# Gradients of four interleaved layers on one core: sums behind a block, loads in another order, three banks for small transposes

## The chip, the cores and the metric

The kernel runs on one core of a Trainium2 chip. The metric is device time in microseconds (us) of one execution; before the change the median of three runs is 1201.8 us (1201.69 to 1202.94). Its engines are named as in the profile: PE (TensorE, matmuls and transposes), DVE (VectorE), ACT (ScalarE), POOL (GpSimd) and SP (SyncE, which here issues DMA transfers). Accumulators of PE lie in PSUM banks, all other tiles on the chip in SBUF; DRAM holds inputs, outputs and what is saved for the gradients.

## The reference: what is computed

Input x has 2048 rows of 512, in bfloat16. Four layers follow one another, each adding to x, and the kernel returns the output and the gradients of all inputs for a given grad_out:

```python
x = x + A(layernorm(x))      # layer 0
x = x + B(layernorm(x))      # layer 1
x = x + A(layernorm(x))      # layer 2, same weights
x = x + B(layernorm(x))      # layer 3, same weights
# A: qkv = h @ wqkv; 32 heads of 16; phi(t) = where(t > 0, t + 1, exp(t)) + 1e-6
#    kv = phi(k)^T v; z = sum phi(k); o = phi(q) kv / (phi(q) z + 1e-6); o @ wo
# B: h = sigmoid(h @ w_gate) * (h @ w_up); h @ w_down       (inner width 1376)
out, vjp = jax.vjp(f, x, wqkv, wo, w_gate, w_up, w_down)
return out, *vjp(grad_out)
```

## The kernel before, in words

**Stages.** The forward layers take the first 430 us or so; they save to DRAM what the gradients need (tensors named sv_...). The gradient stages come in this order, with their approximate times in the profiled execution: `BBwd` of layer 3 (433 to 556 us), `ABwd.first` of layer 2, called A2.first (556 to 638), `ABwd.second` of layer 2 (638 to 716), the rest of layer 3's weight-gradient units and the start of layer 1 (to 780), `BBwd` of layer 1 (780 to 899), A0.first (899 to 980), A0.second (980 to 1060), then small transposes and weight-gradient units that are left (to the end, 1198).

**BBwd** (from L1166; `run` from L1287 on). The 2048 rows are four blocks of 512 (`NBLK`), the inner width of 1376 is eleven units of 128 (`NFC`; the last is 96). For unit n = 11 B + u:

- `D(n)`: four matmuls make the gradient of the inner product, dhh_ps (L1241), in one of two PSUM banks; ACT casts it to the tile dhb (L1247), DVE multiplies the PSUM with one saved factor (L1248) and POOL dhb with the other (L1249), which gives dd. The saved factors ssd are loaded per group of two or three units.
- `R(n)`: once a group is complete, DVE transposes dd in blocks (L924, 1.5 us each) and SP stores it as sv_hdd or sv_hdl, for the weight gradients later.
- `H(B, u)`: eight matmuls (L1273) add the unit's share to the four accumulators dh_ps of the block.
- `ln_begin(B)` follows the last unit of a block. For each accumulator ACT writes t_sb (L1101), DVE makes a sum (tile junk, L1120) and POOL a small factor ab; only then are the four accumulators free. Later steps of the LayerNorm gradient (add_t, add_r) are spread over the next block's units.

`D` runs two units ahead of `H` (`LOOK`). At the beginning of layer 3 the first units' tiles come from an earlier pool (names pre_...), because they are made before `run` opens its pools; dhb of the units in `run` comes from pool bb_work, whose memory the last forward stores (out_t) used. At the end of `run`, `nxt.gT_make`, `nxt.dp_make` and `nxt.start` do the first steps of the ABwd stage that follows, and `next(fill)` issues a fill unit.

**Fill units.** `p_set` holds a set of operands of weight gradients (rows of sv_hdd, sv_hdl or sv_dqk, 1 to 1.5 MB, two buffers), `p_a` the other operand of the whole length. A unit is 16 matmuls (p_ps, L1511). Its result goes through dw_stg (DVE L1526 or ACT L1528) to a partial sum in DRAM (dwp_...) or to the output, in the last case through transposes wd_tp (L1486). Fill units stand between the steps of ABwd so that PE has work while other engines work.

**ABwd.first** (L1597). For each of 16 tiles of 128 rows: `dp_make` (L1582, four matmuls), `gT_make` (L1574), `cneg_make`, `dq_ops` on DVE (L1637 to L1643), `accum_dz`, and a fill unit (every fourth tile two for layer 0). `dq_ops` multiplies with the saved query factors, tile phq_ld (256 KB for two tiles, three buffers, loaded through `BatchLoader`, L1153), and overwrites them; after each pair `dqk_store` stores them as sv_dqk in two DMAs (L1543). At its start `load_a_weights` (L243) issues loads of X_Nv (0.5 MB), wqkvT (1.5 MB) and woT (0.5 MB); they are used in `second`, and their tiles share memory with layer B's weights. GT (L1679 ff.) is written into half of the last one. pqn loads follow (three of 0.5 MB), then phq_ld. For layer 2, `b_load_all` loads a2 (p_a, 2 MB in four DMAs) when `open_a2` is called, ahead of `first`; for layer 0 the call stands ahead of A0.first likewise.

**Small transposes** (`a_small_transposes`, L1822): ten groups of four transposes (four of G, four of X, two of kvbd and dkvbd), each group through a tile fin_ps in the single bank "ln", copied out by ACT and DVE in turn (L362, L364), then four stores.

**What orders the work.** In the gradient stages `tc.manual_schedule(engines=EM)` keeps PE, ACT, DVE and POOL in the order in which the Python code issues instructions; SP is not in it, and its DMAs are put in order by the scheduler, with `tc.issue_after(ins)` as a bound. SP has one queue in order: a store that waits for its data holds all loads behind it. At most eight DMAs are outstanding (each issue waits for the landing of the eighth before).

## Time and profile before

| | |
|---|---|
| Median of the runs | 1201.8 us (1201.69 to 1202.94, 3 runs) |
| Profiled execution, its own time | 1199.77 us |
| Span of that execution | 1198.1 us |
| Mean granted clock of PE | 0.994 |
| DMA traffic | 258.18 MB, mean 216 GB/s |

By stretch, us of busy time in the profiled execution:

| Stretch, us | PE | DVE | ACT | POOL | clock | DMA share |
|---|---|---|---|---|---|---|
| 425 to 570, block stage of layer 3 | 137.95 of 145 | 97.54 | 58.80 | 85.81 | 0.99 | 0.80 |
| 570 to 640, A2.first | 68.67 of 70 | 47.96 | 29.98 | 8.74 | 1.00 | 0.73 |
| 640 to 780, A2.second and rest | 138.41 of 140 | 52.92 | 65.75 | 3.07 | 1.00 | 0.67 |
| 780 to 912, block stage of layer 1 | 128.53 of 132 | 92.60 | 64.09 | 83.87 | 1.00 | 0.77 |
| 912 to 985, A0.first | 67.66 of 73 | 52.72 | 28.77 | 8.45 | 1.00 | 0.81 |
| 985 to 1060, A0.second | 74.32 of 75 | 50.37 | 45.39 | 13.37 | 1.00 | 0.48 |
| 1060 to 1076, small transposes | 13.70 of 16 | 3.70 | 4.08 | 0.00 | 0.89 | 0.79 |
| 1076 to 1198, units left | 116.58 of 122 | 26.21 | 7.79 | 0.00 | 0.99 | 0.77 |

A row says how long an engine had instructions running in that stretch. "Clock" is the share of full speed that PE was granted. In lines of the timeline, the bracket at the end tells how long the engine was idle ahead of the instruction and what ended that time; in lines of waits the numbers are total us, times, and the longest.

### The profile page before, as it was taken

The numbers are of one execution on the slowest core, as the hardware profiler recorded it, in microseconds if no ns is written. First come the engines' busy times: TensorE is split into PE (matmuls) and PEld (weight loads), VectorE is DVE, ScalarE is ACT, GpSimd is POOL, SyncE is SP. The second block draws the span as 40 slices with busy tenths as digits, with TensorE's granted clock in tenths as the row PEclk, the third lists the DMA queues.
The fourth block names the chain that finished last, engine by engine and source line by source line (L and its number), as shares of the span: only waits on it lengthen the run. The fifth ranks groups of instructions, "written<-read, shape, count | busy, mean of one in ns | idle before, by whom it ended". The sixth has DMA issues, their size and how long they took to land. (4 is left out here: it accounts for less than half of the span.)

```text
span 1198.1 us, 21274 instructions
## 1 busy us (share of the span) xinstructions
PE 1139.9 (95%) x7958; PEld 699.2 (58%) x8066; DVE 739.8 (62%) x1275; ACT 569.0 (47%) x1039; POOL 412.8 (34%) x578
## 2 busy tenths in 40 slices
PE   7989999997999989999999999999999989999998
PEld 4467776446777644445555556744447645556577
DVE  6688887877767557767684760066777946732221
ACT  5666666546676623444545652245545427620001
POOL 4237775204766435774110000047771101100000
PEclk9999999999999999999999999999999999999999
DMA  7934566534556666879865439987769874459875
GB/s 241 311 121 147 174 192 190 172 131 141 174 168 215 203 224 216 299 225 332 286 219 155 141 107 311 304 305 224 232 203 334 269 229 145 150 175 312 271 209 165
DMA packets 282184, 258.18 MB, mean 216 GB/s; under 512 B 29216, under 2 KB 261600, under 8 KB 280928
## 3 DMA queue, kind: packets, MB, share of 16 engines
q1 hardware_dynamic: 282080, 256.82, 67.0%
q8 instruction: 63, 1.03, 0.3%
q14 instruction: 41, 0.34, 0.1%
HBM read 137.30 MB, written 119.47 MB: 214 GB/s over the span
## 5 line engine op out<-in xcount | busy, mean ns | idle before, releaser
L1511 PE MATMUL p_ps<-p_set,p_a 128*128 128x384 bf16 (+2 forms) x1792 | 268.9, 305 | 7.7 <-DMA p_set<-sv_hdd 3.3
L1511 PEld LDWEIGHTS <-p_a 128*128 128x128 bf16 x1792 | 168.8, 96 | 89.7 <-issue 5.4
L1249 POOL TENSOR_TENSOR dd<-dhb,ssd 128x512 bf16<-128x512 bf16 x85 | 98.2, 1156 | 122.4 <-ACT dhb L1247 120.1
L1248 DVE TENSOR_TENSOR dd<-dhh_ps,ssd 128x512 bf16<-128x512 f32 x85 | 57.6, 678 | 121.0 <-ACT dhb L1247 119.7
L1273 PE MATMUL dh_ps<-wuT,dd 128*128 128x512 bf16 (+1 forms) x340 | 129.0, 379 | 2.9 <-DVE junk L1120 2.0
L972 POOL TENSOR_TENSOR ssd_t<-hhT,oms 128x512 bf16<-128x512 bf16 (+1 forms) x92 | 97.9, 1070 | 75.0 <-DVE hhT L971 30.8
L1273 PE MATMUL dh_ps<-wgT,dd 128*128 128x512 bf16 (+1 forms) x324 | 122.9, 379 | 0.0
L1273 PEld LDWEIGHTS <-dd 128*128 128x128 bf16 x680 | 66.3, 98 | 83.7 <-issue 5.2
L1247 ACT CAST dhb<-dhh_ps 128x512 bf16<-128x512 f32 x86 | 50.3, 587 | 122.2 <-PE dhh_ps L1241 105.2
L955 PE MATMUL g_ps<-hT,wg 128*128 128x256 bf16 (+1 forms) x792 | 93.5, 262 | 1.2 <-DVE hT L362 1.2
L955 PE MATMUL u_ps<-hT,wu 128*128 128x256 bf16 (+1 forms) x792 | 93.3, 262 | 0.5 <-DVE hhT L971 0.5
L1526 DVE TENSOR_TENSOR dw_stg<-p_ps,dw_stg 128x384 bf16<-128x384 f32 (+2 forms) x76 | 32.1, 438 | 99.8 <-PE p_ps L1511 99.4
L924 DVE STREAM_TRANSPOSE tr_stg<-dd 128x768 f32<-128x768 f32 (+1 forms) x62 | 86.8, 1436 | 3.6 <-DMA sv_hdd<-tr_stg 1.7
L971 DVE TENSOR_TENSOR hhT<-u_ps,ssd_t 128x512 bf16<-128x512 f32 (+1 forms) x92 | 57.7, 631 | 49.7 <-ACT ssd_t L969 37.5
L969 ACT ACTIVATE ssd_t<-g_ps 128x512 bf16<-128x512 f32 (+1 forms) x92 | 51.9, 564 | 66.3 <-PE g_ps L955 51.9
L1241 PE MATMUL dhh_ps<-gT,wdT 128*128 128x512 bf16 x302 | 78.3, 379 | 2.0 <-ACT gT L1213 1.1
L987 PE MATMUL y_ps<-wd,hhT 128*128 128x512 bf16 (+1 forms) x337 | 78.7, 380 | 0.8
L955 PEld LDWEIGHTS <-wg 128*128 128x128 bf16 x792 | 69.6, 99 | 16.6 <-issue 0.8
L955 PEld LDWEIGHTS <-wu 128*128 128x128 bf16 x792 | 71.2, 99 | 7.6 <-issue 0.7
L1528 ACT CAST dw_stg<-p_ps 128x384 bf16<-128x384 f32 (+2 forms) x76 | 28.1, 386 | 80.7 <-PE p_ps L1511 76.7
L1241 PEld LDWEIGHTS <-wdT 128*128 128x128 bf16 x352 | 34.0, 98 | 44.9 <-issue 6.9
L987 PEld LDWEIGHTS <-hhT 128*128 128x128 bf16 (+1 forms) x352 | 34.3, 98 | 35.3
(263 smaller groups left out, 2067.4 us busy)
## 6 DMA issues: line engine op xcount, KB each, us to landing
sv_hdd<-tr_stg SPq DMA_DIRECT2D x72, 384.0 KB, 3.8
p_set<-sv_hdd SPq DMA_DIRECT2D x18, 1536.0 KB, 7.2
sv_ssd<-ssd_t SPq DMA_DIRECT2D x74, 256.0 KB, 2.4
ssd<-sv_ssd SPq DMA_DIRECT2D x23, 768.0 KB, 4.8
p_set<-sv_dqk SPq DMA_DIRECT2D x8, 1024.0 KB, 6.9
h_ld<-sv_h SPq DMA_DIRECT2D x30, 256.0 KB, 4.0
sv_hdl<-tr_stg SPq DMA_DIRECT2D x24, 256.0 KB, 4.5
p_a<-sv_h SPq DMA_DIRECT2D x12, 512.0 KB, 6.8
```

What stands on the lines that cost most here:

```text
L924: nc.vector.transpose(t[:, :, 0:n * P].bitcast(F32).rearrange("p q (a j) -> p q a j", a=2 * n), src.rearrange("p c x -> p (c x)").bitcast( ...
L955: nc.tensor.matmul(ps[:, ci * n:(ci + 1) * n], lhsT=w_sb[:, kc, (c0 + ci) * P:(c0 + ci + 1) * P], rhs=hT[:, kc, (st % 2) * P:(st % 2) * P ...
L969: nc.scalar.activation(ssd[:, :, 0, :], gv, ACT.Sigmoid)
L971: nc.vector.tensor_tensor(hh, uv, ssd[:, :, 0, :], ALU.mult)
L972: nc.gpsimd.tensor_tensor(ssd[:, :, 1, :], hh, oms, ALU.mult)
L987: nc.tensor.matmul(y_ps[:], lhsT=h[0:r, fc, off:off + P], rhs=k.wd[0:r, fc, :], start=(fc == 0), stop=(fc == NFC - 1))
L1241: nc.tensor.matmul(ps[:], lhsT=k.wdT[:, jc, u * P:(u + 1) * P], rhs=self.gT[B][:, jc, :], start=(jc == 0), stop=(jc == NDC - 1))
L1247: nc.scalar.copy(dhb[:], ps[:])
L1248: nc.vector.tensor_tensor(self.dd[ng][:, 0, c, :], ps[:], self.ssd[ng][:, c, 0, :], ALU.mult)
L1249: nc.gpsimd.tensor_tensor(self.dd[ng][:, 1, c, :], dhb[:], self.ssd[ng][:, c, 1, :], ALU.mult)
L1273: nc.tensor.matmul(self.acc[j][:], lhsT=dd[0:r, a, c, j * P:(j + 1) * P], rhs=w[0:r, u, :], start=(u == 0 and a == 0), stop=(u == NFC - 1 ...
L1511: nc.tensor.matmul(ps[:, 0:w], lhsT=lhs[:, s, ic * P:(ic + 1) * P], rhs=rhs, start=(s == 0), stop=(s == NST - 1))
```

## The change

Nothing that is computed changes, and no matmul is added or removed; instructions stand in another order, and some tiles in other memory.

- In `D`, units n below 4 of the layer-3 stage put dhb into the earlier pool (pre_dhb).
- `run` makes `D` and `R` of one more unit ahead of the loop. At a block's end the sums (`ln_begin`) follow `H` directly, then two units of `D`; `R` comes behind. In layer 3, block 2, unit 9, `D` follows `H`.
- At the end of `run`: sums of tiles 0 and 1, a fill unit, sums of tiles 2 and 3, then `gT_make(1)`.
- In `first`, phq_ld tiles are loaded by `load_ph` (two pairs ahead of the loop, then two pairs early), pqn behind them, a2 behind the first pqn, and `load_a_weights` at tile 4, behind the factors issued last.
- `a_small_transposes` takes the banks "t", "ln", "t" in turn ("t" has two).

```diff
         def open_a2(l):
             k.a2ctx = ExitStack()
-            ectx = k.a2ctx if l == 3 else bctx
-            k.a2 = b_load_all(k, R, k.sv[l]["gbf"], "p2_a2", ectx.enter_context(
-                tc.tile_pool(name=f"a2_{l}", bufs=1, reuse_waits="tile")))
+            pool = (k.a2ctx if l == 3 else bctx).enter_context(
+                tc.tile_pool(name=f"a2_{l}", bufs=1, reuse_waits="tile"))
+
+            def load():
+                k.a2 = b_load_all(k, R, k.sv[l]["gbf"], "p2_a2", pool)
+            k.load_a2 = load
...
-        if self.p["work"] is None:
+        if self.first and n < 4:
             dhb = k.pre["pool"].tile([P, BT], BF16, name="pre_dhb")
...
-    def ln_begin(self, B):
+    def ln_begin(self, B, js=range(NB)):
...
             for n in range(self.LOOK):
                 self.D(n)
                 self.R(n)
+            self.D(self.LOOK)
+            self.R(self.LOOK)
...
-                    self.D(n + self.LOOK)
-                    if end and u == NFC - 1:
+                    close = u == NFC - 1
+                    behind = self.first and B == 2 and u == 9
+                    if close and end:
                         nxt.gT_make(0, "ln")
+                    if not close and not behind:
+                        self.D(n + self.LOOK)
                     self.H(B, u)
-                    self.R(n + self.LOOK)
+                    if behind:
+                        self.D(n + self.LOOK)
+                    if close and not end:
+                        done = self.ln_begin(B)
+                        for i in range(2):
+                            self.D(n + self.LOOK + i)
+                    if u:
+                        self.R(n + self.LOOK)
+                    if close and not end:
+                        self.R(n + self.LOOK + 1)
...
-                if end:
-                    nxt.gT_make(1, "ln")
-                lns = self.ln_begin(B)
+                if not end:
+                    lns = done
+            lns = self.ln_begin(B, (0, 1))
             next(fill)
+            lns += self.ln_begin(B, (2, 3))
+            nxt.gT_make(1, "ln")
...
-        k.load_a_weights(l)
...
-            phld = BatchLoader(k, stg, sv["phq"], "phq_ld", nb=NB2)
+            phs = {}
+
+            def load_ph(i):
+                if i < NST // NB2:
+                    phs[i] = stg.tile([P, NB2, D], BF16, name="phq_ld")
+                    phs["ins"] = nc.sync.dma_start(out=phs[i][:], in_=dram_batch(sv["phq"], i, NB2)).ins
...
-            for b in range(1, NST // NB):
-                nc.sync.dma_start(out=self.pqn[b][:], in_=dram_batch(sv["pqn"], b))
+            load_ph(0)
+            load_ph(1)
+            with tc.issue_after(phs["ins"]):
+                for b in range(1, NST // NB):
+                    ins = nc.sync.dma_start(out=self.pqn[b][:], in_=dram_batch(sv["pqn"], b)).ins
+                    if b == 1:
+                        with tc.issue_after(ins):
+                            k.load_a2()
             for st in range(NST):
-                ph_st = phld.get(st)
-                T = dict(st=st, ph=ph_st, ph_pair=phld.cur)
+                if st % NB2 == 1:
+                    load_ph(st // NB2 + 2)
+                if st == 4:
+                    with tc.issue_after(phs["ins"]):
+                        k.load_a_weights(l)
+                    GT = k.GT
+                T = dict(st=st, ph=phs[st // NB2][:, st % NB2, :], ph_pair=phs[st // NB2])
...
-        ps = ps_tile(k, "ln", [P, NDC, P], BF16, "fin_ps")
+        ps = ps_tile(k, ("t", "ln", "t")[n % 3], [P, NDC, P], BF16, "fin_ps")
```

In the built order of the changed program, SP's queue in both first stages reads: query factors, pqn, a2 (p_a), the other pqn, p_set, stores of dqk, factors, X_Nv, wqkvT, woT, p_set. At the end of layer 0 nine groups of small transposes stand with two fill matmuls among them.

More of the change, by code (lines that the diff above doesn't have):

```diff
@@ L1274, in H @@
                                  start=(u == 0 and a == 0), stop=(u == NFC - 1 and a == 1))
-    def ln_begin(self, B):
+    def ln_begin(self, B, js=range(NB)):
         k, l = self.k, self.l
         out = []
-        for j in range(NB):
+        for j in js:
             st = B * NB + j
@@ L1283, in ln_begin @@
                              rs, k.xs[st], self.G[B][:, j, :] if self.first else None, bufs=4))
-            out[j].sums_ps(self.acc[j][:], rs)
+            out[-1].sums_ps(self.acc[j][:], rs)
         return out
@@ L1606, in first @@
         small = self.small = ctx.enter_context(tc.tile_pool(name=f"ab_small{l}", bufs=6, reuse_waits="tile"))
-        GT = k.GT
         self.dkvbdT = big.tile([P, NDC, P], BF16, name="dkvbdT")
```

## The prediction, on record

> **What bounds the kernel now.** I began with the page: busy times, then the span in slices.

> ```profile
> PE 1139.9 (95%) x7958; PEld 699.2 (58%) x8066; DVE 739.8 (62%) x1275; ACT 569.0 (47%) x1039; POOL 412.8 (34%) x578
> ...
> PEclk9999999999999999999999999999999999999999
> ```

> PE is busy 95% of 1198.1 us. The change adds and removes no matmul, so only PE's idle time (58 us) and what it runs slowly can change; no other engine is near its limit. Second view, PE's waits (line of the waiting matmul, releaser, total us, times, longest):

> ```profile
> PE dhh_ps L1241 <- DVE pre_dd L1248: 3.6, 1, 3.6
> PE p_ps L1511 <- DMA p_set<-sv_hdd: 3.3, 2, 2.6
> ...
> PE dh_ps L1273 <- DVE junk L1120: 2.0, 7, 0.5
> ...
> PE p_ps L1511 <- ACT dw_stg L1528: 1.2, 2, 1.0
> PE dhh_ps L1241 <- ACT gT L1213: 1.1, 1, 1.1
> ```

> Those five are in the gradient stages, which begin at 425 us. "Idle before" starts when the modelled last matmul ends, up to 0.17 us after its array slot; I therefore price a wait by the distance of matmul starts less a matmul's own pitch (0.216 us for 512 columns). Priced so, the gaps over 0.25 us from 425 us on, with a 0.2 us part of some, sum to about 25 us: 3.81 at 437.71; 0.63 (once 0.84), in two parts, at each of six block boundaries (469, 499, 530, 813, 843, 873); 1.26 at 522.41; 0.39 at 560.03 and 1.18 at 902.15; 1.05 at 580.74; 0.95, 1.14, 2.72 and 0.66 at 921.38, 952.24, 959.47 and 965.11; 2.86 among the small transposes at 1066 to 1069; the other 4.7 lie where the change moves nothing.

> Third view, busy time in stretches (PE busy and instructions, granted clock, DMA share, GB/s), PE alone:

> ```profile
> 438.70:442.10 3.40, 0.37 (x2) 1.00 1.05 395
> 442.10:445.50 3.40, 3.40 (x10) 0.50 0.75 248
> 1066.80:1070.20 3.40, 1.53 (x19) 0.99 0.81 240
> 1070.20:1073.60 3.40, 3.40 (x16) 0.51 0.68 212
> 70.10:73.50 3.40, 2.30 (x25) 1.00 0.23 83
> 957.50:960.90 3.40, 2.29 (x14) 1.00 1.03 374
> ```

> **Part by part**, against the profiled execution (1199.77 us: span 1198.1 and 1.67 around it).

> *1. The cast of dhh (L1247) into a tile of the earlier pool for units 2 and 3.*

> ```profile
> 440.37 1.07 ACT L1247 CAST dhb<-dhh_ps 128x512 bf16<-128x512 f32 x2 [10.10 <-DMA out_dram<-out_t]
> ...
> 441.73 1.56 PE L1241 MATMUL dhh_ps<-pre_gT,wdT 128*128 128x512 bf16 x4 [3.65 <-DVE pre_dd L1248]
> ```

> ACT waits until the last store of the forward output has left the memory that the dhb tile reuses (landed 440.22); PE, with two banks for dhh, is then held through DVE. In the changed program units 2 and 3 cast into the old pool, and unit 4 is first to meet the same landing, at 440.4; PE wants its bank back for unit 6, about 443.1 (unit 4's dhh would stand near 437.9, and a unit's 12 matmuls take 2.6 us). Covered: -3.8, and with it the halved clock at 442.1, -1.7. **-5.5.** If something else holds units 2 and 3 (the ssd factors land at 438.61), about 1 us comes back.

> *2. Block boundaries.* The LayerNorm sums (ACT t_sb 0.69, DVE junk 0.75, four of each) hold the four accumulators that the next unit's first matmuls want, and before them DVE has two dhh products (0.68 each). Changed: sums go first, and PE has two dhh units (2x0.86 us) before it needs a bank. Next late would be GpSimd's product (1.16 each), ready 3.85 us after the boundary against wanted 4.32, and the second dhh bank, 3.1 against 3.46. Six boundaries by 0.63: **-3.8**, bounds 0 (margin of 0.36 gone) and -4.4.

> *3. One unit's dhh behind its accumulation (B=2, u=9).* The 1.26 us at 522.41 is dhh waiting for ACT's gT copy; 8 matmuls (1.73 us) now stand between. **-1.2.**

> *4. End of a run.* The first fill unit goes between sums 0,1 and 2,3, and gT_make(1) behind. That takes the wait for dw_stg (ACT L1528) at 560.03 and 902.15, where sums stand ahead of the copy on ACT and DVE: -0.3 and -1.0. LayerNorm's last add stays where it was on DVE (568 and 910 us). **-1.3**; bounds 0 and -1.6.

> *5. Query factors ahead, weights at tile 4.* SyncE issues every DMA in one in-order queue, and transfers run one behind another (0.5 MB 1.45 us, 1.5 MB 4.5). So each waiting store blocks all loads behind it.

> ```profile
> 579.71 0.69 DVE L1639 SCALAR_TENSOR_TENSOR phq_ld<-phq_ld,rden_all 128x512 bf16<-128x512 bf16 x1 [8.69 <-DMA phq_ld<-sv_phq]
> ```

> A2.first: DVE idles 8.69 us and PE then 1.05 at 580.74. The factors now land near 571: -1.05. But in the changed order the second and third p_set of weight-gradient operands come behind a dqk store that waits for DVE; working the queue through they land about 586.3 (wanted 585.5) and 601.7 (wanted 601.5): together +1, bounds 0 and +2. **0.**

> A0.first: before, PE waits 0.95 at 921.38 for p_set<-sv_dqk, behind 2.5 MB of weights; now that set comes ahead: -0.95. The weights then stand behind dqk store 1, which waits for DVE's dq_ops of tile 3, about 924.0 (927.96 before, less the 3.93 us that DVE idles at 919.5 for its factors). The transfer queue is empty from 919 to about 926; then 0.25 (factors), 2.5 (X, wqkvT, woT) and 1 MB (the next p_set) are 10.5 us of transfers: landed 937 to 938. Before, that set was issued at 920.48 and landed 928.71; PE first reads it at 932.88, changed 2.1 earlier, 930.8. **PE gets a new wait of 6.7 us**; bounds 4.5 (weights overlap with the store's wait) and 8. It is as sparse as the rows above: +1.7. DVE, ahead by 4 us and with PE held, has no backlog any more: the 1.14 at 952.24 (DVE dw_stg) goes, and the p_set that lands late at 959.47 is asked for earlier, -2.7. **+3.6**; bounds 0 and +8.8 (nothing regained).

> *6. Small transposes in three PSUM banks.* With one bank each group of four (0.22 us of PE) waits for the copy ahead: pitches of 1.06 (ACT copy, 0.58) and 0.90 us (DVE copy, 0.42). With three, three groups share a 1.06 us cycle: 0.35 each. In the changed order nine groups stand with two fill matmuls at A0's end: about 1.2 us idle in place of 2.86 and some 0.6 of smaller gaps: -2.3; A2's end, where fills cover, -0.4. The window ahead of 1070.2 would be some 65% busy, like the 2.30-of-3.40 row, so no halved clock: -1.6. **-4.3**; bounds -1.5 and -5.5.

> [...]

> **Sum:** -5.5 -3.8 -1.2 -1.3 +0 +3.6 -4.3 = -12.5, so 1187.3 for a run like the profiled one. The median of the runs is 2.0 above that (1201.8 against 1199.77), which I keep: **1189.3 us**.

> **Rivals.**

> *A. No new wait in A0.first* (DVE reaches tile 3 sooner, or the store's wait overlaps with enough transfers). For it: DVE needs only 3.1 us a tile. Against: store 1 needs both tiles, and tile 3's dp comes at PE's pace. 12.5+8.4 = 20.9: 1180.9. Chance 0.14.

> *B. The queue costs more than it gives.* +2 in A2.first, 8+1.7 in A0.first, 1.14 and 2.72 not regained, the clock at 1070 still halved: -11.8+0.95+8.75-2.7 = -4.8: 1197.0. For it: PE waits for p_set even now. Against: DVE's backlog, their cause, is gone. Chance 0.19.

> [...]

> *D. Slower.* The same mechanism in both first stages: where the 2.5 MB of weights issued at tile 4 delay a p_set, PE stands still and the clock halves. Gains elsewhere are 16.1 and regained waits up to 5.9 more; parity needs A2.first and A0.first to lose 16 to 22 us together, twice 8 to 11. It takes one more set in each stage late by the weights' 7 us, since the two sets' buffers free one another. For it: 1.5 MB sets that land within a microsecond of need in A2.first. Against: DMA is busy only 0.73 there (570 to 640 us), so later sets recover. At 27 us lost and 5.9 regained: -16.1 -5.9 +27 = +5.0, 1206.8. Chance 0.09.

> *E. The change doesn't do what it says* (unit 4's cast holds PE as unit 2's did, boundaries keep a wait through GpSimd): 1199 to 1203. Chance 0.05.

> **How the numbers follow.** Forecast (within 3 us of 1189.3) 0.40, A 0.14, B 0.19, C 0.13, D 0.09, E 0.05. The range goes from A's neighbourhood, 1181.5, to B's upper side, 1198, leaving out D, E and about 0.06 of A. 0.2% (2.4 us) is about what a measurement of this kernel can tell from no change. Faster by more: forecast, A, B, C and a little of E, 0.86; within: 0.05; slower: D, 0.09.

> **What the changed profile would show.** Right: no wait for pre_dd near 438 and clock 1.00 after it; no "junk" releaser for dh_ps; DVE's idle for phq_ld under 3 us in A2.first; one p_ps wait of 5 to 8 us for p_set<-sv_dqk in A0.first near 915 to 930, with wqkvT landing just before it; fin_ps pitches near 0.35. Wrong: waits of PE for p_set in A2.first over 2 us, a dhh_ps wait on GpSimd at boundaries, no wait at all in A0.first, or 3.4 us at clock 0.50 behind the small transposes.

## The result, and the profile after

The changed kernel takes 1205.35 us (median of 7 runs, 1202.95 to 1208.88), the kernel before 1201.8 (7 runs on the same chip, 1197.93 to 1202.94): ratio 1.0043, 95% interval 1.0026 to 1.0059. It is slower, by 5.2 us going by the ratio and by 3.6 going by the medians; 12.5 faster was forecast. The profiled execution took 1204.04 us, its span 1202.3 us against 1198.1.

The page of the changed kernel, busy times and granted clock:

```profile
PE 1139.5 (95%) x7958; PEld 700.4 (58%) x8066; DVE 740.2 (62%) x1275; ACT 568.7 (47%) x1039; POOL 411.7 (34%) x578
...
PEclk9999999999999999999999999999999899999999
```

PE does the same work. What differs stands in its waits (us in total, times, longest); lines of this kernel are some 3 to 33 higher than before (L1511 is now L1530):

```profile
PE p_ps L1530 <- DMA p_set<-sv_dqk: 7.8, 2, 7.1
PE p_ps L1530 <- DMA p_set<-sv_hdd: 7.8, 4, 4.0
...
PE wd_tp L1505 <- ACT dw_t L1508: 2.1, 1, 2.1
...
PE dh_ps L1276 <- DVE dd L1251: 1.4, 1, 1.4
```

The waits for pre_dd (3.6), junk (2.0), gT (1.1) and dw_stg (1.2) that the change aimed at are gone. In their place PE waits 16.2 us for p_set (0.6 of it for sv_hdl), 4.9 before. Behind three of these waits the clock is at 0.50, as the last three of these stretches show (length, PE busy, granted clock, DMA share, GB/s):

```profile
441.30:444.70 3.40, 3.40 (x18) 1.00 1.08 366
1066.90:1070.30 3.40, 3.29 (x40) 1.00 0.77 214
937.30:944.10 6.80, 2.81 (x14) 0.50 0.95 325
582.30:585.80 3.50, 3.35 (x11) 0.51 0.68 197
725.70:729.10 3.40, 3.40 (x13) 0.50 1.05 396
```

The first stretch was at 0.50 before, and the second holds the small transposes, behind which 0.50 was granted before; both stretches and what follows the second have the full clock now. The three others are new.

Following the same matmul through both traces gives each stage's share (us, minus is faster):

| Stage | Forecast | Measured | Where |
|---|---|---|---|
| to 445 us: cast into the old pool | -5.5 | -5.3 | as forecast |
| to 555: boundaries, unit behind | -3.1 | -0.2 | -2.5 gained, +2.3 lost at 545 |
| to 640: end of run, A2.first | -0.3 | +3.5 | p_set 2.26 and 1.08 late, clock 0.50 for 3.41 us |
| to 725: A2.second, small transposes | -0.4 | +5.6 | p_set 4.19 late, clock 0.50 for 3.41 us |
| to 895: block stage of layer 1 | -1.9 | -1.4 | 0.26 is left at each boundary |
| to 982: end of run, A0.first | +2.6 | +4.1 | p_set 7.29 late (6.7 forecast), clock 0.50 for 6.83 us |
| to the end | -3.9 | -2.0 | transposes as forecast; wd_tp 2.29 late |
| sum | -12.5 | +4.3 | |

**What stands ahead of the late loads.** SyncE's queue of the changed kernel at A2's end, and PE's wait:

```profile
713.36 0.36 SPq L1871 DMA_DIRECT2D sv_G<-G  x1
714.98 0.36 SPq L1871 DMA_DIRECT2D sv_XT<-XT  x1
715.43 0.52 SPq L1871 DMA_DIRECT2D sv_kvbd<-kvbd  x1
716.05 0.97 SPq L1871 DMA_DIRECT2D sv_dkvbd<-dkvbd  x1
717.11 0.51 SPq L1431 DMA_DIRECT2D p_set<-sv_hdd  x1
```

```profile
725.26 4.94 PE L1530 MATMUL p_ps<-p_set,p_a 128*128 128x384 bf16 x19 [4.03 <-DMA p_set<-sv_hdd]
```

The same place in the kernel before:

```profile
714.08 0.36 SPq L1412 DMA_DIRECT2D p_set<-sv_hdd  x1
716.88 0.36 SPq L1838 DMA_DIRECT2D sv_G<-G  x1
```

There p_set went ahead of the store of G. With three banks the copies end sooner, and the scheduler puts all four stores ahead of the load: SyncE waits for the copies to G and XT (7.8 and 1.2 us), and 1.3 MB of stores go ahead on the transfers too (landed from 716.33 to 719.55). The set lands at 725.13 instead of 720.62; PE wants it at 721.

A0.first is as the prediction worked it out: store 1 of dqk holds the queue to 925.90, then X_Nv, wqkvT and woT go (927.35 to 930.48), and the set behind them is issued at 930.52 and lands at 941.25:

```profile
941.29 3.30 PE L1530 MATMUL p_ps<-p_set,p_a 128*128 128x256 bf16 x16 [7.13 <-DMA p_set<-sv_dqk]
```

### The profile page after: what moved, and what is told of

Same layout as the page of the kernel before. It is cut to its first block, busy times and chain, and to the rows that moved or that the text cites. A ratio compares the mean times of both kernels' runs of the same rounds, so it can differ in the third digit from the quotient of the medians.

```text
span 1202.3 us, 21276 instructions
## 1 busy us (share of the span) xinstructions
PE 1139.5 (95%) x7958; PEld 700.4 (58%) x8066; DVE 740.2 (62%) x1275; ACT 568.7 (47%) x1039; POOL 411.7 (34%) x578
## 3 DMA queue, kind: packets, MB, share of 16 engines
q8 instruction: 63, 1.03, 0.4%
## 5 line engine op out<-in xcount | busy, mean ns | idle before, releaser
L1530 PE MATMUL p_ps<-p_set,p_a 128*128 128x384 bf16 (+2 forms) x1792 | 270.6, 307 | 17.5 <-DMA p_set<-sv_dqk 7.8
L1530 PEld LDWEIGHTS <-p_a 128*128 128x128 bf16 x1792 | 170.4, 97 | 101.9 <-issue 11.4
L975 POOL TENSOR_TENSOR ssd_t<-hhT,oms 128x512 bf16<-128x512 bf16 (+1 forms) x92 | 97.9, 1069 | 75.1 <-DVE hhT L974 32.6
L1104 ACT ACTIVATE t_sb<-dh_ps,rstd_all 128x512 f32<-128x512 f32 x64 | 43.6, 687 | 28.9 <-issue 12.6
```

The source lines that it names most:

```text
L975: nc.gpsimd.tensor_tensor(ssd[:, :, 1, :], hh, oms, ALU.mult)
L1530: nc.tensor.matmul(ps[:, 0:w], lhsT=lhs[:, s, ic * P:(ic + 1) * P], rhs=rhs, start=(s == 0), stop=(s == NST - 1))
```

## The experiments

Theory Q: a load that stands behind something else in SyncE's queue costs what it lands late; undone one by one, the gains are there. Theory T: the transfers as a whole limit these stages, and PE waits elsewhere for what it gained. Every ratio below is against the kernel before, run on the same chip in the same job (its medians 1202.0 to 1203.3). The changed kernel (1205.35, ratio 1.0043) was measured in another job. Where a difference to it is given below, it is one of medians; by the ratios no_factors_first gains 8.4 us on it in place of 6.7, no_three_banks 5.5 in place of 3, a2_early 6.2 in place of 5.5, and weights_at_start loses 6.2 in place of 10.5.

| Run | Median, us | Ratio (95%) |
|---|---|---|
| no_factors_first | 1198.65 | 0.9973 (0.9956 to 0.9991) |
| no_three_banks | 1202.40 | 0.9997 (0.9985 to 1.0010) |
| neither | 1196.76 | 0.9957 (0.9941 to 0.9974) |
| banks_alone | 1204.93 | 1.0023 (1.0010 to 1.0036) |
| cast_alone | 1194.46 | 0.9922 (0.9898 to 0.9947) |
| sets_opened_later | 1195.79 | 0.9934 (0.9912 to 0.9956) |
| stores_behind_set | 1193.68 | 0.9917 (0.9894 to 0.9940) |
| weights_at_start | 1215.81 | 1.0095 (1.0068 to 1.0123) |
| weights_at_tile_10 | 1208.97 | 1.0061 (1.0037 to 1.0086) |
| a2_early | 1199.90 | 0.9991 (0.9973 to 1.0008) |
| cast_banks_stores_behind | 1195.58 | 0.9947 (0.9934 to 0.9961) |
| order_alone | 1200.61 | 0.9990 (0.9977 to 1.0004) |
| order_repaired | 1190.62 | 0.9908 (0.9890 to 0.9927) |
| all_repaired | 1191.65 | 0.9916 (0.9892 to 0.9940) |

### Three banks

banks_alone is the kernel before with one line changed, no_three_banks the changed kernel without it:

```diff
-        ps = ps_tile(k, "ln", [P, NDC, P], BF16, "fin_ps")
+        ps = ps_tile(k, ("t", "ln", "t")[n % 3], [P, NDC, P], BF16, "fin_ps")
```

> The kernel before with the small transposes in three banks and nothing else. Theory Q: its SyncE queue has the four stores ahead of p_set as the changed kernel has, so a wait of about 4 us appears near 723 us and one of about 2 us near 1078, and the gain among the transposes is 4: 2 to 4 us slower than before, 1204 to 1206. Rival S: no new wait, 3 to 4 us faster than before, 1198.

> The changed kernel with the small transposes in the single bank again. Theory Q (with three banks the four stores of the small matrices come ahead of a p_set load in SyncE's queue, and ahead of the stores of dw_t): the 4.2 us wait for p_set at the end of A2.second goes with its half clock, and the 2.3 us wait of wd_tp; the 4.4 us among the transposes come back: 3 to 4 us faster than the changed kernel, 1201 to 1203. Rival S (the wait at the end of A2.second comes from the load order in A2.first, which shifts the units): the wait stays, and the kernel is 3 to 4 us slower than the changed one.

banks_alone is 2.0 us slower than before. Its queue, and PE:

```profile
719.58 0.97 SPq L1838 DMA_DIRECT2D sv_dkvbd<-dkvbd  x1
720.65 0.51 SPq L1412 DMA_DIRECT2D p_set<-sv_hdd  x1
```

```profile
728.70 2.65 PE L1511 MATMUL p_ps<-p_set,p_a 128*128 128x384 bf16 x11 [3.93 <-DMA p_set<-sv_hdd]
```

It has the 4 us wait with nothing else of the change in it, so the load order in A2.first is not its cause. In no_three_banks p_set is issued at 715.21, ahead of the store of G (718.01), and PE doesn't wait there; it is 3 us below the changed kernel. Q holds on both. Up to 640 us this program issues the same DMAs in the same order as the changed kernel, yet the two waits in A2.first are 3.40 and 3.05 us where the changed kernel has 2.26 and 1.08: a wait of this kind, read from one execution, is good to 1 or 2 us. The repair issues the four stores behind the next load (the rest of that helper, and its call later, left out):

```diff
+    def finish(self):
+        with self.k.tc.issue_after(self.R.dmas[-1]):
+            a_small_stores(self.k, self.l, self.small_T)
...
         A2.second()
+        w3.take(4)
+        A2.finish()
```

> The run no_factors_first (block stages and three banks) with the four stores of the small matrices issued behind the next p_set load. Theory Q: the 4.2 us wait for p_set at 716 and its half clock go, the three banks' gain stays: 4 to 7 us faster than no_factors_first, 1191.5 to 1195. Rival T: the 1.3 MB of stores cost the same wherever they stand: 1197 to 1199.5.

```profile
709.83 0.36 SPq L1434 DMA_DIRECT2D p_set<-sv_hdd  x1
710.71 0.36 SPq L1483 DMA_DIRECT2D dwp_wd<-dw_stg  x1
711.16 0.77 SPq L1869 DMA_DIRECT2D sv_G<-G  x1
```

The wait at 716 is gone, and the kernel is 5.0 us below no_factors_first, as Q had it. A wait of 2.03 us for the copy to dw_t remains at 1063: one buffer, whose store (issued 1057.15, landed 1061.93) stands behind four p_set loads. With the cast but without the new block order the banks bring nothing:

> The kernel before with pre_dhb, three banks, and the four stores of the small matrices behind the next p_set load; block order and load order as before. If the parts add: cast_alone's 8.8 us and some 2 to 4 of the banks: 1190 to 1192.5. If the banks' gain is given back to waits for transfers: 1194 or more.

1195.58, against 1194.46 for the cast alone: the 2.9 us of gaps among the transposes are gone, and a wd_tp wait of 2.56 us stands in their place; the clock is at 0.50 afterwards in both (from 1064.8 us in cast_alone and from 1066.7 here). "If the parts add" falls.

### Load order of the first stages

no_factors_first undoes this part of the diff; neither undoes it and the banks:

> The changed kernel with its load order in the two first stages put back as before (factors, pqn, a2, weights). Theory Q (SyncE's in-order queue: the late weights hold back p_set): the waits of 2.3, 1.1 and 7.3 us for p_set in A2.first and A0.first and the half clock behind them go, the old waits of 1.05, 0.95 and up to 3.9 come back: 8.5 us faster than the changed kernel, about 1195 to 1198, and below the kernel before. Rival T (transfers as a whole are the limit, so that PE merely waits elsewhere for what it gained): within 2 us of the changed kernel, 1203 to 1206.

> The block stages' part of the change alone: pre_dhb, sums ahead of two units of dhh, the unit behind, the order at the end of a run; load order and bank as before. Theory Q: all five losses go, and what is left is the gain of the block stages, 8 to 9 us: 1192 to 1195. Rival T: the 8.8 us gained by 545 us are given back at later waits for transfers: 1198 to 1201.

Undone, it gives back 6.7 us beside the banks and 5.6 without them (1202.40 against 1196.76). The waits of 7.29, 2.26 and 1.08 us are gone. no_factors_first ends 0.65 us above the range that Q gave; neither, at 1196.76, lies between Q (1192 to 1195) and T (1198 to 1201). Three runs change one thing each in the changed kernel, in this order weights_at_tile_10, weights_at_start and a2_early (where the call behind the first pqn goes as well):

```diff
-                if st == 4:
+                if st == 10:
```

```diff
-                if st == 4:
-                    with tc.issue_after(phs["ins"]):
+                if st == 0:
+                    with tc.issue_after(ins):
```

```diff
             def load():
                 k.a2 = b_load_all(k, R, k.sv[l]["gbf"], "p2_a2", pool)
-            k.load_a2 = load
+            load()
```

> The changed kernel with load_a_weights at tile 0, behind the last pqn load, and the factors still ahead of all. Theory Q: it is the weights behind dqk store 1, not the factors ahead, that holds p_set back: the waits of 2.3, 1.1 and 7.3 us go, nearly all of the 6.7 us between the changed kernel and no_factors_first come back, 1197 to 1200. Rival U (any order with factors first delays p_set): 1203 to 1206.

> The changed kernel with one number changed: load_a_weights at tile 10 instead of 4. Theory Q (the weights hold up the p_set behind them): the wait of 7.3 us in A0.first with its 3.4 us more of half clock, and the 1.1 us in A2.first, go; the 2.3 us wait at 580 in A2.first, ahead of the weights, stays: 7 to 10 us faster than the changed kernel, 1195.5 to 1198.5. Rival V (the weights are as much in the way of a later set): 1201 to 1205, with a new wait of 4 us or more for p_set<-sv_hdd near 950.

> The changed kernel with the 2 MB load of a2 issued ahead of the factors, as before. Theory G (the first factor tile's memory comes free only with LayerNorm's last add, so SyncE and the transfers stand idle for some 8 us at 554 to 562; what comes behind is late by that): the 2.3 us wait at 580 and the half clock behind it go, A0.first keeps its 7.3: 3.5 to 5 us faster than the changed kernel, 1200.5 to 1202. Without G: no difference.

weights_at_start is the miss of the study: 10.5 us slower than the changed kernel, where I expected 5 to 8 faster, and above rival U's range as well. PE's waits:

```profile
PE p_ps L1530 <- DMA p_set<-sv_hdd: 16.5, 4, 10.9
PE p_ps L1530 <- DMA p_set<-sv_dqk: 8.6, 1, 8.6
```

So it is not the weights at tile 4 alone. The queue of the changed kernel shows the other half:

```profile
551.38 0.58 SPq L1229 DMA_DIRECT2D h_ld<-sv_h  x1
562.71 0.87 SPq L1642 DMA_DIRECT2D phq_ld<-sv_phq  x2
```

From 552 to 562.7 SyncE issues nothing: the first factor load waits until LayerNorm's last add on DVE (561.89 to 562.6; the profile puts 10.7 us of SyncE's waiting down to it), and everything else of the stage is behind it. Before, X_Nv, a2 and wqkvT went out in that time (from 557.09). a2_early fills the gap with 2 MB of a2:

```profile
550.92 2.06 SPq L1462 DMA_DIRECT2D p_a<-in_grad_out_dram  x4
561.51 0.88 SPq L1642 DMA_DIRECT2D phq_ld<-sv_phq  x2
```

It is 5.5 us faster than the changed kernel; A2.first has no wait for p_set left, and the one in A0.first is 4.55 instead of 7.13. G holds. weights_at_tile_10 does what Q said at its place (the set lands at 932.99, no wait at 934), and then loses more than that, for the next set stands behind the weights, a2 parts (p_a) and stores in turn:

```profile
969.83 4.82 PE L1530 MATMUL p_ps<-p_set,p_a 128*128 128x384 bf16 x16 [10.75 <-DMA p_set<-sv_hdd]
```

Rival V had the mechanism right: the 2.5 MB only choose which set is late. Its place (near 950) and its time (1201 to 1205) were off, for the wait ends at 969.8 us after 10.75, and the 16 matmuls behind it take 4.82 us, where 16 of them took 2.79 at 956.28.

### Cast and block order

cast_alone is the one line in `D`; order_alone is the diff of `ln_begin` and `run`; sets_opened_later adds to neither:

```diff
-        B3.run(A2, {(1, 8): open_a1, (3, 1): open_sets})
+        B3.run(A2, {(1, 8): open_a1, (3, 4): open_sets})
```

> The kernel before with pre_dhb for units 2 and 3 and nothing else. Theory Q: the 3.8 us wait at 437.7 and the half clock behind it go and nothing is late next before 780 us: 4.5 to 5.5 us faster than before, 1197 to 1198. Rival T (what PE gains it loses again where it waits for transfers): half or more is given back by the end, 1199.5 or more, with larger p_set waits than before at 916 and 950 us.

> The kernel before with the new order of the block stages alone (sums ahead of two units of dhh, the unit behind, end of a run), without pre_dhb. Theory Q: 3 to 4 us faster than before, 1199 to 1200. Theory T (what the block stages gain is given back at the ssd load near 550 us and at p_set loads): within 1 us of before, or slower by up to 2, since cast_alone was 2.3 us faster than cast and order together.

> The run named neither (block stages' part alone) with the first two p_set loads of layer 3 (3 MB) opened at unit 4 of the last block instead of unit 1, so that the last load of ssd factors is not behind them in SyncE's queue. Theory Q: the 1.8 us wait for dd at 545.6 and the half clock after it go, 2 to 4 us faster than neither: 1193 to 1195. Rival T: the same bytes are late elsewhere, above all the first fill unit near 551: no difference, 1196 to 1198.

cast_alone is 8.8 us faster than before, more than forecast. Its trace shows the forecast part: span 1193.3, 4.8 below before, with the wait at 437.7 and the halved clock gone. The other 4 us no trace here shows: the profiled execution of before (1199.77) lies 3.5 us below the median of this job's runs of it, that of cast_alone 0.5 above its own. A lower mean clock in those runs of before (0.9926 against 0.994 in the profile) makes up 1 to 2 us of the 3.5 by my estimate (0.0014 of 1198 us is 1.7); the rest is open. order_alone gains 1.4 us, within its interval of nothing and near what T said (within 1 us); Q said 3 to 4. But T's reason is only half right. In the run neither, the last load of ssd factors stands behind two sets of 1.5 MB and lands at 546.81:

```profile
534.44 1.43 SPq L1428 DMA_DIRECT2D p_set<-sv_hdd  x2
535.98 0.70 SPq L1222 DMA_DIRECT2D ssd<-sv_ssd  x1
```

```profile
547.65 0.39 PE L1273 MATMUL dh_ps<-wuT,dd 128*128 128x512 bf16 x1 [1.65 <-DVE dd L1248]
```

Before, PE came there 7 to 9 us later, and the load was in time but for 0.53 us of DVE. In sets_opened_later the ssd load (535.27) is ahead of the second set, and the wait is gone; the median falls by 1.0 us only, with 2.45 us (1.66 in neither) waited for a set near 767 and the clock at 0.50 behind that wait and one at 916 (mean clock of the profile 0.992, 0.995 in neither). The last two runs take the pieces together:

> The run stores_behind_set (all of the change but the load order of the first stages, stores behind the set) with the first two p_set loads of layer 3 opened at unit 4 of the last block. Theory Q (only a transfer that stands in the wrong place costs time): the 1.8 us at 543.9 goes, 1 to 3 us faster than stores_behind_set, 1190.5 to 1192.5. Theory T (the p_set near 767 us lands when it lands, whenever PE gets there): the wait for it near 765 us grows by as much as is gained at 544, and the time stays at 1193 to 1195.

> The whole change, factors first and weights at tile 4 included, with three repairs: a2 loaded ahead of the factors, the small stores behind the next set, the first two sets opened at unit 4. If the three repairs add to what a2_early showed (1199.9): the 4.2 us at 715 with its half clock and the 1.6 us at 544 go, the 4.7 us in A0.first stays: 1191 to 1194, no better than order_repaired.

order_repaired (cast, block order, three banks, stores behind the set, sets opened later; load order as before) has the lowest median here, 0.9908 of before and 3.1 us below stores_behind_set; by the intervals cast_alone, stores_behind_set and the two repaired kernels can't be told apart, by the spans they stand at 1193.3, 1190.5, 1188.5 and 1188.9. The wait near 765 is 0.83 us (1.78 there), and that set landed at 764.90 instead of 767.16: it moves with PE, so T's fixed landing time falls. all_repaired keeps the factors first and a wait of 4.85 us in A0.first, and is no faster.

## Why the prediction was wrong, step by step

- **1, the cast:** right. -5.3 against -5.5; ACT meets the landing at unit 4 and PE doesn't feel it (ACT casts at 440.23 after 3.38 us of waiting for out_t).
- **2, boundaries:** right in kind, too large. The second dhh bank was said to be free 0.36 us ahead of need; PE waits 0.26 us for it (dhh_ps on DVE's dd) at five of the six, 0.60 at the other. Gain about 0.4 each, not 0.63.
- **3 and 4:** the unit behind and the end of the run took their waits away. Missing was the next thing late: the ssd load behind two sets, 1.5 us at 545 and 0.7 behind it.
- **5, A2.first:** wrong. The 1.05 us went, but "together +1" for two sets was +3.3 and a halved clock. I carried the landing times without setting them against PE's new, earlier time at the same units: the sets landed 3.9 and 1.3 us ahead of the times in the working (582.41 and 600.36), PE wanted them 5.3 and 2.2 us ahead.
- **5, A0.first:** right mechanism, right size: 7.29 us against 6.7. Nearly all of the old 0.95 stayed (0.81). The clock was at 0.50 for 6.83 us and not for 3.41, but PE was busy in 0.00 of the first 3.40 us (937.30:940.70); behind it 16 matmuls took 3.30 us, where 16 of them take 1.91 at full clock (before, 932.88), so it cost 1.4 us and not more than the 1.7 forecast. The 2.7 became 0.87 (now a wait for DVE's t_t). Together +4.9 for +3.6.
- **6, three banks:** the transposes gained as forecast, 0.2 to 0.5 us a group. The failed step is "A2's end, where fills cover, -0.4": I costed PE, ACT and DVE and left out the four stores that the copies release. Moved ahead of a load in SyncE's queue they cost 4.19 us and a halved clock at A2's end. At A0's end PE waits 2.29 us for the copy to dw_t, whose store lands behind them (issued 1072.63, landed 1077.21); that is not theirs alone, for 1.7 to 2.6 us stay in the four runs that issue them later, where four p_set loads stand ahead. This is the largest error, 8 us; with step 5's 3.8 in A2.first and 1.3 in A0.first and the 2.3 at 545 it is most of the 17 us between forecast and trace.
- **The halved clock at 1070:** gone, as said. The stretch with the transposes has PE busy in 3.29 of its 3.40 us (1066.90:1070.30; some 65% was forecast, 1.53 of 3.40 was measured before), and the 3.40 us that follow are at 1.00. The clock also stayed at 1.00 behind the 2.29 us for dw_t's copy, where 0.50 followed 2.56 us in cast_banks_stores_behind.
- **Rivals:** A fell (there was a wait). C did not occur: the clock was at 1.00 behind the small transposes (1070.30:1073.70). B and D came nearest: D's mechanism, sets late in both first stages, was there (3.3 and 8.1 us of waits), but it took the small stores, which no rival named, to end on the slower side.

## What to carry to other kernels

When an engine is made faster or earlier, list every DMA that its results release and every load that is wanted at a fixed place behind them in the same in-order queue: a store that comes free sooner can pass a load that nothing had moved. Set each transfer's new landing time against the new time at which it is wanted, since a stage that gains 8 us also wants its loads 8 us sooner. A load that must wait for memory should not stand first in a queue: here SyncE issued nothing for 10.7 us, the transfers stood idle for 7.6 of them (DMA share 0.00 from 555.1 to 562.7), and moving 2 MB into that gap was worth 5.5.

## What the runs showed of the hardware

From 425 us on, the trace of the changed kernel has the clock at 0.50 for 3.41 us from 582.34 and from 725.70, and for 6.83 us from 937.33. PE was busy in 1.40, 0.44 and 0.27 of the 3.40 us ahead of these. The wait for dw_t's copy (2.12 us, to 1078.37) lies in the two stretches at 1073.70 and 1077.10, and 1.00 follows both:

```profile
578.90:582.30 3.40, 1.40 (x13) 1.00 1.06 371
582.30:585.70 3.40, 3.25 (x11) 0.51 0.67 195
722.30:725.70 3.40, 0.44 (x3) 1.00 1.03 375
725.70:729.10 3.40, 3.40 (x13) 0.50 1.05 396
933.90:937.30 3.40, 0.27 (x8) 1.00 1.15 373
937.30:940.70 3.40, 0.00 (x0) 0.50 0.98 374
940.70:944.10 3.40, 2.81 (x14) 0.50 0.93 277
1073.70:1077.10 3.40, 2.55 (x16) 1.00 0.83 233
1077.10:1080.50 3.40, 2.13 (x16) 1.00 0.79 238
1080.50:1083.90 3.40, 3.40 (x36) 1.00 1.01 338
```

In the run neither, 0.50 followed a stretch in which PE was busy for 1.61 us, with a wait of 1.65 us in it; 1.00 followed one in which it was busy for 2.32 us, with 24 transposes among its 26 matmuls:

```profile
70.70:74.10 3.40, 2.32 (x26) 1.00 0.42 147
74.10:77.50 3.40, 2.74 (x51) 1.00 0.58 205
545.20:548.60 3.40, 1.61 (x7) 1.00 1.06 365
548.60:552.00 3.40, 3.40 (x12) 0.50 0.88 286
```

The columns are length, PE busy (matmuls), granted clock, DMA share and GB/s. So the length of a wait alone does not tell the clock behind it in these runs: 0.50 followed 1.65 us, and 1.00 followed 2.12.
